# A state-space convolution with an MLP on one core: one PSUM pool for all stages, the first MLP block's sums in the searched order, and a new order

## The chip, the core and the metric

One core of a Trainium2 chip runs the whole program. The metric is the time of one execution on the device in microseconds; lower is better. The engines are PE (matmul), DVE (vector), ACT (scalar), POOL (GpSimd) and SP, whose queue mostly issues transfers; each works through its own queue in order and waits on the others by semaphores.

## What is computed

Two layers on a sequence of 2048 rows with 512 channels, with a layer normalisation ahead of each.

```python
# A: diagonal state space, applied as a long convolution
dt = exp(log_dt); logdA = dt * (A_re + 1j*A_im)
K  = real(sum_n C[d,n] * exp(logdA[d,n] * l) * dt*B[d,n])      # 512 x 2048 filter
y  = irfft(rfft(u, 4096) * rfft(K, 4096))[:2048] + u * Dskip
h  = x + y(layernorm(x))
# B: MLP, F = 1376
out = h + gelu(layernorm(layernorm(h)) @ w1 + b1) @ w2 + b2
```

## The kernel before

The kernel never forms the filter by 128 x 2048 exponentials per channel. It builds two small tables per half of the channels, multiplies them into the filter, and does the Fourier transforms as matmuls with tables of sines.

Stages, in the order in which they begin:

- `params`, `tables`, `norm_in` (lines 322 to 789): sines and cosines in `M`, turned copies in `R` and `Rn` by transposing DMAs, the layer normalisation of `x` (`st` are its sums, `u` the normalised rows). Each of 16 row groups is multiplied by a block-diagonal table (`aps`, line 780), copied from PSUM to SBUF (`a`, line 784) and written to DRAM (`A_dram`, line 789).
- `exps`, `p_half`, `q_half` (602 to 691), once per half of the channels: exponentials on ACT into `Pt` (the tile `both`) and `Q`; phases by matmul (`pv`, `qv`), their sines on ACT (`s`, `sq`, line 118), products on DVE.
- `kgen` (694): four blocks per half, each of 128 small matmuls of 128x32 by 20 columns (line 707, `kps`), a copy on ACT (`ku`) and two sums on DVE (`near`, `far`). These go to DRAM and come back as `kt` (lines 732 to 739). The second half's exponentials write over what the first half's `kgen` reads.
- `x_load`, `x_stage` (792 to 825): `A_dram` is read back as `X` in four loads, and 16 steps of 8 matmuls (`xps`) finish its spectrum in place.
- `conv` (828): for each half 8 pairs of frequencies; 22 matmuls (`kfps`, lines 848 and 850), a copy (`kf`), four products on DVE (`pa`, `pb`), 8 matmuls (`zps`, 873 to 876), a copy (`z`), a write to DRAM (`Zd`) and a return in another layout (`both<-Zd`, line 888). The last pair of the second half is done in two parts.
- `early_rows` (955): the first 256 channels of the convolution's result, by `first_half` (line 930, `y`), with the input row added and sums for the normalisation (`first_sums`).
- `mlp` (987): four blocks of 512 rows. `y_mm` and `y_sums` do the other 256 channels; `scale` normalises (`y2`); `turn` transposes, in block 0 on PE (`tps`, line 1047) and later by DMA; `up` makes 11 pieces of the hidden layer (`h1ps`, line 1055: four matmuls, then the GELU on ACT, line 1057, into `hT`); `down` makes an output tile of 128 rows (`o2ps`, line 1067: 11 matmuls, then the residual add on DVE into `ot`, and a write). In block 0 the ups run twice over 256 columns, elsewhere once over 512.

What sets the order: everything ahead of `mlp` is recorded as steps in a planner (`Sched`, line 121), with an engine, a cost and dependencies each. The list `ORDER` (line 31), found by a search outside the program, says in which order the steps are issued; where a step may run on two engines (copies from PSUM on ACT or DVE), the lowest bit of the entry says on which. `mlp` is written out by hand and begins after the last step. Every wait between engines is put in by the framework from the tiles that the instructions touch.

PSUM has eight banks of 512 fp32 columns. Ahead of `mlp` one pool holds three buffers of two banks (tag `p`) and one (tag `q`, for `zps`). It is closed, and `mlp` opens its own pool, in which each of the tags `yps`, `o2ps`, `tps` and `h1ps` has two tiles in turn:

```python
pt = ps1.tile([P, 512], f32, name="h1ps")
...
pt = ps1.tile([P, 512 // parts], f32, name="o2ps", tag="o2ps")
```

Of the kernel before, what the change touches and what calls it, by code (L numbers as in the profile page):

```python
# [31 lines left out]
    110, 4, 24, 28, 8, 32, 40, 6, 38, 42, 36, 126, 140, 66, 142, 144, 44, 156, 68, 58, 124, 118, 22, 114, 86, 116, 88, 72, 296, 128, 278, 152, 164, 294, 280, 90, 276, 298,  # L32
    136, 292, 130, 70, 160, 122, 132, 284, 168, 120, 300, 112, 270, 138, 288, 48, 272, 178, 74, 290, 148, 286, 274, 134, 76, 60, 78, 80, 46, 166, 282, 50, 170, 188, 302, 10,
    52, 180, 174, 190, 54, 335, 434, 62, 56, 12, 173, 184, 82, 176, 254, 252, 92, 183, 262, 258, 476, 186, 470, 478, 464, 472, 480, 482, 94, 336, 466, 474, 338, 500, 454,
    468, 502, 340, 484, 96, 504, 192, 98, 488, 194, 494, 490, 100, 506, 486, 102, 508, 436, 496, 344, 106, 492, 438, 346, 456, 84, 348, 440, 414, 158, 405, 416, 350, 150,
    445, 512, 14, 418, 154, 162, 458, 420, 146, 554, 460, 510, 514, 548, 556, 524, 516, 498, 550, 536, 560, 558, 526, 552, 562, 530, 528, 196, 532, 538, 534, 198, 566, 564,
    518, 540, 568, 16, 200, 520, 446, 570, 19, 542, 202, 448, 522, 406, 544, 206, 450, 578, 408, 374, 208, 424, 212, 410, 546, 572, 224, 218, 230, 236, 242, 216, 584, 574,
    576, 222, 580, 582, 234, 586, 590, 588, 240, 246, 376, 592, 684, 718, 426, 379, 594, 380, 228, 698, 596, 704, 720, 700, 248, 354, 708, 384, 356, 686, 429, 696, 386, 314,
    688, 430, 359, 316, 716, 600, 714, 324, 364, 692, 326, 389, 694, 360, 734, 329, 366, 390, 710, 394, 330, 304, 706, 319, 690, 712, 369, 306, 320, 726, 396, 399, 370, 702,
    722, 756, 309, 400, 730, 728, 738, 310, 750, 724, 758, 736, 732, 740, 760, 744, 604, 752, 608, 786, 742, 612, 746, 792, 616, 754, 788, 780, 794, 748, 822, 782, 768, 796,  # L40
    824, 790, 810, 784, 770, 652, 826, 812, 798, 655, 800, 828, 772, 830, 656, 840, 658, 802, 620, 814, 842, 834, 623, 836, 804, 832, 680, 806, 844, 774, 682, 838, 628, 808,
    776, 624, 631, 846, 626, 778, 762, 848, 668, 764, 850, 636, 670, 766, 672, 638, 816, 674, 644, 882, 818, 852, 647, 820, 664, 854, 856, 892, 666, 676, 894, 640, 678, 896,
    660, 642, 858, 662, 898, 860, 862, 632, 900, 928, 634, 902, 864, 930, 932, 906, 648, 866, 910, 878, 650, 868, 870, 934, 912, 964, 936, 914, 938, 874, 916, 966, 946, 918,
    968, 920, 970, 948, 942, 1000, 972, 950, 886, 974, 924, 1054, 1002, 1004, 952, 978, 1056, 1036, 954, 1058, 956, 1006, 1038, 982, 1008, 1040, 1010, 960, 1060, 984, 1090,
    1062, 986, 1064, 1014, 1042, 1092, 1072, 1044, 1094, 1046, 1068, 1096, 1074, 1126, 1098, 1100, 1050, 988, 1128, 1076, 1018, 990, 992, 1104, 1130, 1078, 1020, 1108, 1080,
    1022, 1082, 996, 1132, 1110, 1162, 1134, 1112, 1136, 1024, 1164, 1086, 1180, 1026, 1166, 1028, 1114, 1182, 1184, 1116, 1144, 1140, 1118, 1168, 1146, 1032, 1171, 1186,
    1148, 1188, 1172, 1190, 1122, 1150, 1200, 1152, 1176, 1212, 1202, 1194, 1154, 1208, 1214, 1204, 1158, 1210, 1198, 1206
# [274 lines left out]
def tables(nc, S, K, cp, mp, cv, ct, c2, psp, dram):  # L322
# [117 lines left out]
    for k in (0, 8):  # L440
        def flip(k=k):
            nc.sync.dma_start_transpose(out=K.R[:, k:k + 8].rearrange("p k c f -> p (k c) f"), in_=K.M[:, 0, k:k + 8].rearrange("p k c f -> p (k c f)"))

        ends.append(S.dma("SP", 1.3, flip, [K.o_m[0]], 1.2, lat=1.8))
    K.o_rn = S.dma("SP", 1.3, lambda: nc.sync.dma_start_transpose(out=K.Rn[:], in_=K.Mn.rearrange("p k f -> p (k f)")), [K.o_mn], 1.2, lat=1.8)
# [3 lines left out]
def params(nc, S, K, cp, pp, sc, cv, psp, raws, ldt, dtb, grb):  # L449
# [76 lines left out]
    K.o_pl = S.dma("SP", 1.3, turn(src_p, K.PL, 0), [d1], 1.2, lat=1.8)  # L526
# [66 lines left out]
    for h in range(2):  # L593
        K.o_ql.append(S.dma("SP", 1.3, turn(src_q, K.QL, 16 * h), [d5, dq, q1], 1.2, lat=1.8))
# [36 lines left out]
def p_half(nc, S, K, sc, psp, hh):  # L631

    K.o_p, K.o_phs = [[], []], []
    for qd in range(2):
        S.group = f"p{hh}{qd}"
        for g in range(4):
# [22 lines left out]
            x = S.op("ACT", 0.94, sn, [p] + K.o_pe, acq="s", rel=[p], fun=AT["sin"][hh])  # L659
            K.o_p[qd].append(S.op("DVE", 1.23, mul, [x] + K.o_pe, rel=[x]))  # L660


def q_half(nc, S, K, sc, psp, hh):
    K.o_q = [[], []]
    for qd in range(2):
        S.group = f"q{hh}"
        for g in range(5):
# [22 lines left out]
            z = S.op("ACT", 0.94, sn, [x] + K.o_qe, acq="s", rel=[x], fun=AT["sin"][hh])  # L690
            K.o_q[qd].append(S.op("DVE", 0.63, mul, [z] + K.o_qe, rel=[z]))


def kgen(nc, S, K, cv, sc, psp, hh, KD):
    cell = {}
    ends, mm = [], []
    for s in range(2):
        for hv in range(2):
            def mms(s=s, hv=hv):
                Pt, Q = K.Pt, K.Q  # L700
                kps = cell[s, hv] = psp.tile([P, 2, 512], f32, name="kps", tag="p", bufs=PB)
                for i in range(16):
                    for u in range(2):
                        at = 64 * (i % 8) + 32 * u
                        for g in range(4):
                            c = 128 * s + 32 * g + 16 * hv + i
                            nc.tensor.matmul(kps[32 * g:32 * g + 32, i // 8, at:at + 20], lhsT=Pt[:, s, :, u, c - 128 * s], rhs=Q[:, :, u, c], start=True, stop=True, tile_position=(0, 32 * g))  # L707
# [14 lines left out]
            m = S.op("PE", 2.15, mms, K.o_p[s] + K.o_q[s], acq="p")  # L722
            mm.append(m)
            r = S.op("ACT", 0.45, real, [m] + ends, acq="ku")
# [230 lines left out]
def early_rows(nc, S, K, psp, zs, loads):  # L955
    for n in range(4):
# [8 lines left out]
        S.op("DVE", 1.3 if n else 2.8, lambda cell=cell, js=js: first_sums(nc, K, cell["y"][:], 0, js), [m, loads] + K.o_pr0, rel=[m])  # L965
# [21 lines left out]
def mlp(nc, tc, K, ZT, ov):  # L987
    with tc.tile_pool(name="m_sb", bufs=1) as sb, tc.tile_pool(name="m_rot", bufs=2) as rot, tc.tile_pool(name="m_ps", bufs=2, space=PSUM) as ps1:
        warm = sb.tile([1, 1], f32, name="warm")
        nc.scalar.activation(warm[:], K.ones[0:1, 0:1], ACT.Sqrt)  # L990

        def h_of(j, half=None):
            if j < 4:
                v = K.h0[:, j].rearrange("p (h c i) -> p h c i", h=2, c=2)
            else:
                v = K.X[:, j].rearrange("p c d -> p (c d)").bitcast(f32).rearrange("p (c h i) -> p h c i", c=2, h=2)
            return v if half is None else v[:, half]

        def as_h(ap):
            return ap.rearrange("p (h c i) -> p h c i", c=2, i=HW // 2)  # L1000

# [3 lines left out]
        y2, y2T, mv, yps = {}, {}, {}, {}  # L1005
        pairs = (slice(0, 2), slice(2, 4))

        def scale(tb, js):
            n = js.stop - js.start
            ve = rot.tile([P, 4], f32, name="ve2")  # L1010
            ts(nc, ve[:, 0:n], mv[tb][:, js, 1], 1.0 + EPS, ALU.mult, EPS * EPS, ALU.add)
            if not tb and not js.start:
                rs = rot.tile([P, 4], f32, name="rs2")
                nc.vector.reciprocal(ve[:, 0:n], ve[:, 0:n])
                nc.scalar.activation(rs[:, 0:n], ve[:, 0:n], ACT.Sqrt)
                nc.scalar.activation(warm[:], K.ones[0:1, 0:1], ACT.Gelu_apprx_tanh)
            else:
                rs = rsqrt(nc, rot, ve[:, 0:n], n, f"r{n}")
            for jj in range(js.start, js.stop):
                k = jj - js.start  # L1020
                ts(nc, as_h(y2[tb][:, jj, :]), h_of(4 * tb + jj), mv[tb][:, jj, 0:1], ALU.subtract, rs[:, k:k + 1], ALU.mult)

        def tiles(tb):
            mv[tb] = rot.tile([P, 4, 2], f32, name="mv2")
            y2[tb] = rot.tile([P, 4, 512], bf16, name="y2")
            y2T[tb] = rot.tile([P, 4, 4, P], bf16, name="y2T")

        def aggr(tb, js):
            for jj in range(js.start, js.stop):
                nc.vector.bn_aggr(mv[tb][:, jj, :], K.st0[:, 4 * tb + jj, 0:1 if tb else 2].rearrange("p h s -> p (h s)"))  # L1030

        def y_mm(tb, n, tag):
            yp = yps[tb, n] = ps1.tile([P, 2, HW], f32, name="y1", tag=tag)
            first_half(nc, K, yp, 1, slice(4 * tb + 2 * n, 4 * tb + 2 * n + 2))

        def y_sums(tb, n):
            first_sums(nc, K, yps[tb, n][:], 1, slice(4 * tb + 2 * n, 4 * tb + 2 * n + 2))
            aggr(tb, pairs[n])

        def turn(tb, js):  # L1040
            if tb:
                nc.sync.dma_start_transpose(out=y2T[tb][:, js].rearrange("p j c i -> p (j c) i"), in_=y2[tb][:, js].rearrange("p j d -> p (j d)"))
                return
# [198 lines left out]
```

## Time and profile before

| | |
|---|---|
| runs | 305.56 us median of 3 (304.06 to 309.19) |
| the profiled execution | 306.28 us, its span 304.5 us, mean granted PE clock 0.837 |
| busy in the span | PE 251.5 us (83%), DVE 196.6 (65%), ACT 182.7 (60%), POOL 29.7 (10%) |
| X's loads issued / all landed | 102.24 us / 117.1 us |
| first `kgen` on PE | 68.7 to 83.6 us |
| second exponentials on ACT | 85.4 to 101.4 us |
| last `z` copy begins / first `up` of the MLP begins | 201.54 us / 215.55 us |
| MLP: ups of block 0, downs of block 0 | 215.55 to 231.48, to 241.0 us |
| MLP: block 1, block 2, block 3 | to 261.1, to 281.4, to the end |

The page lists busy times first, then the span in 40 equal slices, whose digits are busy tenths. A PE that is counted busy need not run at its peak: the row PEclk beside it says what share of full clock was granted. Times after the chain's start are read from the chain of waits in order of time; the times of single instructions from the groups, where a mean is of one shape only if shapes are kept apart.

### The profile page before, as it was taken

What the parts mean: (1) busy time and instruction counts of PE and PEld (TensorE: products, weight loads), DVE (VectorE), ACT (ScalarE), POOL (GpSimd) and SP (SyncE); (2) the same over time, 40 slices, a digit from 0 to 9 for tenths busy, and PEclk for the clock granted to TensorE, in tenths of its full rate; (3) what the DMA queues carried; (4) which work ended last, traced back from release to release, by engine and by line L of the source; (5) the groups of instructions that cost most, each with busy time, mean ns of one, the idle gap of its engine ahead of it and who ended that gap; (6) DMA issues with size and microseconds to landing.
All of it is one profiled execution on the core that took longest, in us unless ns stands there. A gap on an engine that the chain in (4) does not pass through costs nothing.

```text
span 304.5 us, 5861 instructions
## 1 busy us (share of the span) xinstructions
PE 251.5 (83%) x2318; PEld 147.1 (48%) x2318; DVE 196.6 (65%) x419; ACT 182.7 (60%) x302; POOL 29.7 (10%) x87
## 2 busy tenths in 40 slices
PE   3284897868457589999999999984879999999995
PEld 3221222227411146888777777662565454444443
DVE  4999999996889799531555555657970265473012
ACT  4999899993099998664455555540673161450630
POOL 8100000004020000000411111124000000000000
PEclk9855557595555599999999999978599999999999
DMA  6600096907337692251773554742412104105001
GB/s 167 229 2 0 3 211 141 233 1 187 105 94 229 206 345 86 51 232 58 225 184 122 134 144 141 207 139 54 168 26 63 52 0 103 38 0 121 17 19 52
DMA packets 48901, 34.90 MB, mean 115 GB/s; under 512 B 26441, under 2 KB 46922, under 8 KB 48490
## 3 DMA queue, kind: packets, MB, share of 16 engines
q1 hardware_dynamic: 46810, 23.58, 28.6%
q0 software_dynamic: 2064, 10.95, 11.7%
q8 instruction: 18, 0.29, 0.4%
q14 instruction: 9, 0.07, 0.1%
HBM read 18.58 MB, written 11.22 MB: 98 GB/s over the span
## 4 chain that ended last, share of the span: by engine, by line
PE 58%; DVE 19%; DMA 9%; ACT 7%; issue 5%; SPq 1%; DVEq 0%; ACTq 0%; POOLq 0%
PE h1ps L1055 13%; PE kfps L850 13%; PE o2ps L1067 12%; PE kps L707 6%; DMA X<-A_dram 4%; DVE st L764 3%; DVE w L70 2%; ACT sq L118 2%; DVE both L70 2%; PE kfps L848 2%; DVE a L82 2%; ACT hT L1057 1%; PE aps L780 1%; PE zps L874 1%; DMA M<-in_A_A_re_dram 1%
## 5 line engine op out<-in xcount | busy, mean ns | idle before, releaser
L1057 ACT ACTIVATE hT<-h1ps,b_sb 128x512 bf16<-128x512 f32 (+3 forms) x55 | 32.8, 602 | 43.1 <-PE h1ps L1055 43.1
L1055 PE MATMUL h1ps<-y2T,early 128*128 128x512 bf16 (+3 forms) x220 | 44.5, 351 | 2.7 <-ACT y2T L80 1.8
L850 PE MATMUL kfps<-kt,M 128*128 128x256 bf16 x320 | 40.5, 274 | 0.0
L1067 PE MATMUL o2ps<-w_sb,hT 128*128 128x512 bf16 (+3 forms) x187 | 38.7, 366 | 0.0
L1055 PEld LDWEIGHTS <-early 128*128 128x128 bf16 (+1 forms) x220 | 23.0, 105 | 22.2 <-issue 6.7
L80 ACT CAST kf<-kfps 128x1024 bf16<-128x1024 f32 (+1 forms) x17 | 16.4, 963 | 27.4 <-issue 17.6
L850 PEld LDWEIGHTS <-M 128*128 128x128 bf16 x320 | 28.7, 98 | 6.8
L70 DVE TENSOR_TENSOR pa<-X,kf 128x1024 bf16<-128x1024 bf16 (+1 forms) x17 | 11.2, 661 | 29.1 <-ACT kf L80 29.1
L1067 PEld LDWEIGHTS <-hT 128*128 128x128 bf16 (+1 forms) x187 | 18.2, 98 | 19.7
L70 DVE TENSOR_TENSOR ot<-o2ps,X 128x512 bf16<-128x512 f32 (+1 forms) x13 | 8.4, 650 | 26.5 <-PE o2ps L1067 25.6
L707 PE MATMUL kps<-Q,both 128*32 128x20 bf16 x1024 | 18.6, 221 | 5.5 <-issue 5.5
L70 DVE TENSOR_TENSOR both<-s,both 128x1024 bf16<-128x1024 bf16 x32 | 20.3, 686 | 2.0 <-ACT s L118 2.0
L614 ACT ACTIVATE both<-th 128x256 bf16<-128x256 f32 x64 | 20.6, 400 | 1.7 <-DVE th L70 1.7
L707 PEld LDWEIGHTS <-both 128*32 128x32 bf16 x1024 | 17.8, 169 | 7.5 <-issue 6.7
L780 PE MATMUL aps<-u,BD 128*128 128x512 bf16 x32 | 15.4, 606 | 7.2 <-DVE u L775 5.1
L118 ACT ACTIVATE sq<-qv 128x1024 bf16<-128x1024 int16 x20 | 19.4, 1060 | 0.0
L80 ACT CAST z<-zps 128x1024 bf16<-128x1024 f32 (+1 forms) x16 | 15.8, 989 | 4.3 <-PE zps L876 3.5
L678 PE MATMUL qv<-rows 128*128 128x512 bf16 (+1 forms) x64 | 14.9, 358 | 3.3 <-ACT sq L118 1.9
L644 PE MATMUL pv<-rows 128*128 128x512 bf16 x32 | 13.3, 530 | 5.2 <-ACT s L118 3.6
L118 ACT ACTIVATE s<-pv 128x1024 bf16<-128x1024 int16 x16 | 15.8, 1032 | 0.1
L888 POOL DMA_DIRECT2D both<-Zd x17 | 8.5, 497 | 58.9 <-DMA Zd<-z 42.7
L711 ACT COPY ku<-kps 128x320 f32<-128x320 f32 x8 | 3.4, 446 | 17.6 <-PE kps L707 17.6
(212 smaller groups left out, 440.8 us busy)
## 6 DMA issues: line engine op xcount, KB each, us to landing
A_dram<-a SPq DMA_DIRECT2D x16, 256.0 KB, 2.6
X<-A_dram SPq DMA_DIRECT2D x4, 1024.0 KB, 9.6
Zd<-z SPq DMA_DIRECT2D x15, 256.0 KB, 3.0
both<-Zd POOLq DMA_DIRECT2D x15, 256.0 KB, 3.3
x<-in_A_u_dram SPq DMA_DIRECT2D x4, 512.0 KB, 7.6
rows<-in_A_u_dram POOLq DMA_DIRECT2D x1, 2048.0 KB, 9.1
out_dram<-ot SPq DMA_DIRECT2D x15, 128.0 KB, 1.7
Dp<-Dd POOLq DMA_DIRECT2D x6, 256.0 KB, 5.0
```

The lines of the kernel that those rows point to most:

```text
L70: nc.vector.tensor_tensor(out, a, b, op)
L80: nc.scalar.copy(out, in_)
L118: nc.scalar.activation(out, v.bitcast(i16)[..., 0:2 * n:2], ACT.Sin, scale=S2PI / 65536)
L614: nc.scalar.activation(K.Pt[:, :, k, 1, :], K.th[:, ds].rearrange("p (s c) -> p s c", s=2), ACT.Exp, scale=float(8 * k))
L644: nc.tensor.matmul(v[:, n], lhsT=K.PL[:, b, :], rhs=K.RP[:, 8 * n:8 * n + 8].rearrange("p i c d -> p (i c d)"), start=True, stop=True)
L678: nc.tensor.matmul(v[:, n], lhsT=K.QL[:, b + n, :], rhs=K.RQ[:, m0:m1].rearrange("p i c d -> p (i c d)"), start=True, stop=True)
L707: nc.tensor.matmul(kps[32 * g:32 * g + 32, i // 8, at:at + 20], lhsT=Pt[:, s, :, u, c - 128 * s], rhs=Q[:, :, u, c], start=True, stop=True ...
L780: nc.tensor.matmul(ps[:, h, :], lhsT=K.BD[:, h].rearrange("p a b -> p (a b)"), rhs=cell["u"][:], start=True, stop=True)
L850: nc.tensor.matmul(ps[:, k, c, :], lhsT=K.M[:, t, 2 * k2 + k, c, :], rhs=kt[:, t, :], start=(c == 1 and t == 0), stop=(t == 4))
L1055: nc.tensor.matmul(pt[:fs, 0:n].rearrange("p (a b) -> p a b", b=P), lhsT=K.w1_sb[:, dc, fc * P:fc * P + fs], rhs=y2T[tb][:, js, dc, :], st ...
L1057: nc.scalar.activation(hT[tb % 2][:fs, fc, cols], pt[:fs, 0:n], ACT.Gelu_apprx_tanh, bias=K.b1_sb[:fs, fc:fc + 1], scale=1.0)
L1067: nc.tensor.matmul(pt[:], lhsT=h[:fs, fc, jj * P:(jj + 1) * P], rhs=K.w2_sb[:fs, fc, d], start=(fc == 0), stop=(fc == NFC - 1))
```

## The change

- One PSUM pool. The planner's pool stays open to the end. `mlp` takes four tiles of two banks from it (`o2`, `h1` and `y` with tag `p`, `t` with tag `q`) and `bank()` hands out the two halves of a tile in turn, where it took a new tile from a pool before.
- The first MLP block's start moves into the planner (`first_block`): one group of `y` matmuls for its four row groups, the sums of the first pair of row groups, the sums of the second pair, the root on ACT with the two table loads, and the normalisation of both pairs. The load of ACT's table for the root becomes a step of its own that may come earlier.
- Each `kgen` block of 128 matmuls (256 instructions with the weight loads) becomes two steps of 64.
- The return of the first half's Z waits, in the plan, for all eight of these steps.
- The planner's costs of the transposing DMAs are other numbers.
- `ORDER` is a new list. In it all 16 `A_dram` writes and X's four loads stand ahead of the first `kgen`'s writes on SP; 12 of the 16 `a` copies are on ACT and 4 on DVE (before: 7 and 9); 12 of the 16 `x` steps stand ahead of the second half's phases; the second `kgen` is almost in one piece; the split pair of frequencies is the last of the second half; ACT's table for the root is loaded amid the spectra.
- `w2`'s tile is taken after the new tiles; its loads remain the last step of POOL's queue.

```diff
-def mlp(nc, tc, K, ZT, ov):
-    with tc.tile_pool(name="m_sb", bufs=1) as sb, tc.tile_pool(name="m_rot", bufs=2) as rot, tc.tile_pool(name="m_ps", bufs=2, space=PSUM) as ps1:
+def mlp(nc, tc, K, psp, ov):
+    with tc.tile_pool(name="m_sb", bufs=1) as sb, tc.tile_pool(name="m_rot", bufs=2) as rot:
...
+        for nm, tag in (("o2", "p"), ("h1", "p"), ("y", "p"), ("t", "q")):
+            v = psp.tile([P, 2, 512], f32, name="bank_" + nm, tag=tag, bufs=PB if tag == "p" else QB)
+            banks[nm] = [v[:, n] for n in range(2)]
+
+        def bank(nm):
+            l = banks[nm]
+            l.append(l.pop(0))
+            return l[-1]
...
-                tp = ps1.tile([P, 4, P], bf16, name="tps", tag="tps")
+                tp = bank("t").bitcast(bf16)[:, 0:512].rearrange("p (c i) -> p c i", c=4)
...
-            pt = ps1.tile([P, 512], f32, name="h1ps")
+            pt = bank("h1")
...
-                pt = ps1.tile([P, 512 // parts], f32, name="o2ps", tag="o2ps")
+                pt = bank("o2")[:, 0:512 // parts]
```

```diff
+def first_block(nc, S, K, psp, done, sines_done, rows):
...
+    def sums(n):
+        js = PAIRS[n]
+        first_sums(nc, K, cell["y"][:, js], 1, js)
+        variances(nc, K, K.T0, 0, js)
+        if not n:
+            nc.vector.reciprocal(K.T0.ve[:, js], K.T0.ve[:, js])
...
+    table = S.op("ACT", 1.4, table, sines_done)
+    y = S.op("PE", 1.75, mm, done, acq="p")
+    a = S.op("DVE", 1.8, lambda: sums(0), [y, rows], rel=[y])
+    b = S.op("DVE", 1.7, lambda: sums(1), [y, rows], rel=[y])
+    r = S.op("ACT", 0.35, root, [a, table])
+    S.op("DVE", 0.7, lambda: normed(nc, K, K.T0, 0, PAIRS[0], K.rs0), [r], lat=4.0)
+    S.op("DVE", 1.3, second, [b])
```

```diff
-                for i in range(16):
+                if not part:
+                    cell[s, hv] = psp.tile([P, 2, 512], f32, name="kps", tag="p", bufs=PB)
+                kps = cell[s, hv]
+                for i in range(8 * part, 8 * part + 8):
...
-            m = S.op("PE", 2.15, mms, K.o_p[s] + K.o_q[s], acq="p")
-            mm.append(m)
-            r = S.op("ACT", 0.45, real, [m] + ends, acq="ku")
+            m = S.op("PE", 1.08, lambda mms=mms: mms(0), K.o_p[s] + K.o_q[s], acq="p")
+            m2 = S.op("PE", 1.08, lambda mms=mms: mms(1), [m])
+            mm += [m, m2]
+            r = S.op("ACT", 0.45, real, [m2] + ends, acq="ku")
...
-        ends.append(S.dma("SP", 1.3, flip, [K.o_m[0]], 1.2, lat=1.8))
+        ends.append(S.dma("SP", 2.1, flip, [K.o_m[0]], 1.6, lat=0.8))
...
-    psp = front.enter_context(tc.tile_pool(name="ps", bufs=1, space=PSUM))
+    psp = ctx.enter_context(tc.tile_pool(name="ps", bufs=1, space=PSUM))
```

## The prediction, made before the changed kernel ran

> **What bounds the kernel now.** First the page: span, busy time, slices. Then the chain of waits in order of time, the groups with shapes kept apart, the instructions in order of time around 197 us, and a table of the granted clock in stretches of 2 us.
>
> ```profile
> span 304.5 us, 5861 instructions
> ...
> PE   3284897868457589999999999984879999999995
> ...
> ACT  4999899993099998664455555540673161450630
> ...
> PEclk9855557595555599999999999978599999999999
> ```
>
> Three parts: up to 118 us (slice 15) ACT and DVE are full and PE is held at half clock; from there to 197 us PE is full (filter spectra); from 215 us to the end PE is full again (MLP). Between the last two lie some 14 us of copies and round trips through DRAM.
>
> ```profile
> 225.09 0.61 PE h1ps L1055 x4
> 225.72 0.48 ACT hT L1057
> 226.25 0.61 PE h1ps L1055 x4
> ...
> 231.48 9.51 PE o2ps L1067 x44
> ...
> 244.10 3.53 PE h1ps L1055 x16
> ```
>
> Call the four matmuls of `up` with their GELU an up, the eleven of `down` with their residual add a down. The chain shows how far apart ups are kept: PE 0.61, ACT 0.48, PE 0.61, hand-overs of 0.02 and 0.04. That loop takes 1.16 us and advances two ups (eleven ups take 6.40), because up n waits for the GELU of up n-2: two PSUM buffers. Wide ups (512 columns) don't wait at all: 3.53 / 4 = 0.883 us each; a down takes 9.51 / 4 = 2.38.
>
> ```profile
> L1067 PE MATMUL o2ps<-w_sb,hT 128*128 128x512 bf16 x150 | 34.8, 379 | 0.0
> L1055 PE MATMUL h1ps<-y2T,early 128*128 128x512 bf16 x120 | 28.2, 378 | 0.0
> L1057 ACT ACTIVATE hT<-h1ps,b_sb 128x512 bf16<-128x512 f32 x30 | 20.6, 688 | 37.0 <-PE h1ps L1055 37.0
> ...
> L1057 ACT ACTIVATE hT<-h1ps,b_sb 128x256 bf16<-128x256 f32 x20 | 9.2, 474 | 5.2 <-PE h1ps L1055 5.2
> ...
> L70 DVE TENSOR_TENSOR ot<-o2ps,X 128x512 bf16<-128x512 f32 x11 | 7.6, 691 | 25.1 <-PE o2ps L1067 25.1
> ```
>
> Here are the prices: a wide matmul 378 ns from start to end (216 from start to start), a GELU 688 or 474 ns, a residual add 691.
>
> ```profile
> 197.19 0.69 DVE L82 CAST z<-zps 128x512 bf16<-128x512 f32 x1 [2.22 <-PE zps L876]
> ...
> 197.93 0.27 PE L873 MATMUL zps<-pa,R 128*128 128x256 bf16 x1 [0.78 <-DVE z L82]
> ```
>
> This pair decides the case. The last pair of frequencies is done in halves, and the halves of one `zps` tile lie in different banks. Still the matmul that writes the second bank waits 0.78 us until DVE has read the first. Two banks of one tile are not two buffers.
>
> ```profile
> 58.00:60.00 2.00, 2.00 (x8) 0.50 0.93 312
> 60.00:62.00 2.00, 1.55 (x12) 0.94 0.00 0
> ...
> 66.00:68.00 2.00, 1.62 (x5) 0.77 0.00 0
> ...
> 92.00:94.00 2.00, 1.55 (x4) 0.50 1.02 232
> ```
>
> Columns: PE busy, matmuls, clock, DMA. Half clock ends after 3 to 5 us of nearly dense matmuls (60 us) and comes back after a thin stretch (64 to 66 us). With PE busy for some two thirds or three quarters of the time at half clock (92 us) it stays.
>
> **The change, part by part.** Sums are against the profiled execution: 306.28 us, 1.8 above its span, 0.7 above the median of 305.56.
>
> *One PSUM pool.* `mlp` had five tags with two tiles each. Now it takes four two-bank tiles and hands out their slices in turn. In the built program of the changed kernel the first matmul of every up waits for the GELU of the up just before (before: two back), the first of every later down of a block for the add of the down just before, the second transposes for the copy of the first: as with `zps`. What was overlapped is now in series.
>
> Wide ups: a cycle is 3 x 0.216 + 0.378 + 0.02 + 0.69 + 0.05 = 1.79 instead of 0.883, +0.91 for ten waits in each of blocks 1 to 3. The four `y` groups (0.44) of blocks 1 and 2 now lie in the waits: -1.8. Together 27.3 - 1.8 = +25.5.
>
> Downs: 0.378 - 0.216 + 0.02 + 0.69 + 0.05 = +0.92 per wait, 12 waits = +11.0; the last half of the last, with its 0.42 add, +0.65. Together +11.7.
>
> Ups of block 0 (256 columns, 22 of them): at full clock a cycle is 1.16 instead of 0.58. But before, this stage starts at half clock and leaves it only after 4.9 us of dense matmuls (215.5 to 220.4). In series, at half clock, a cycle is 3 x 0.213 + 0.42 + 0.02 + 0.47 + 0.05 = 1.60, of which 0.85 is PE: 53%, less than in the 92 us row. So I take half clock throughout: 2 x (10 x 1.60 + 0.85) = 33.7, and 2.4 for the second transposes in series: 36.1 against 15.9 (215.55 to 231.48): +20.2. With full clock it would be 26.1: +10.2. The downs that follow start at half clock; until a dense stretch has raised it, about 1.3 of them (2.3 more each): +3, between 0 and +9.
>
> For blocks 1 to 3 the clock is the open point. In series at full clock PE streams 0.864 of 1.79 us, 48%. By the matmuls that the rows list, the stretch 60.3 to 63.7 us had some 45% and kept full clock; 46.6 to 50.0 had 41% of full-height matmuls and lost it. 48% is nearest to the first: full clock. At half clock a cycle is 3 x 0.427 + 0.63 + 0.76 = 2.67, +0.88 for 30 waits, and each block's downs start slowly, 3 x 3: +35. The Trainium skill, "TensorE: Matmul & The Clock Gate", section "A second HAM failure mode: psum-queue depth-cycling", says that small idle times between groups that cycle through PSUM make the clock fall and rise again. By that rule the +35 or a part of it comes; the two stretches just named leave it open, so it is a rival below.
>
> *First block's sums and normalisation in the order.* DVE now does the second pair's sums (0.69 + 0.75 + 0.33 + 0.17 = 1.9) ahead of the first pair's normalisation, and one group of 8 `y` matmuls replaces the first of 4 (0.61): +0.9 at half clock. The Gelu table load (1.28 at 212.91) covers part of it. First GELU input later by +2.5, between +0.5 and +4. The Sqrt table load moves into the spectra, where ACT is half idle (slices 16 to 25): nothing; without that cover 1.3.
>
> *New order, front.* All 16 `a` copies come before kernel generation ends, 12 on ACT (7 before), 4 on DVE (9). X's four loads are issued ahead of the `KD` puts on SP, at about 85 instead of 102.24 us, so the spectra of X are transformed during the second exponentials. But `kgen` of the first half starts 4 us later: DVE does four more `a` copies (1.22), six more `u` (0.37) and one product less (0.60) before it, while the two table sums (1.41, 1.57) move behind: +3.5. `aps`, `qv` stand between its blocks (3 us), so it ends near 90 instead of 83.6. The exponentials, which overwrite its inputs, end near 110 (101.4, +6.4, two X copies of 1.0 between). Then come 24 ACT pieces of about 1.0, then four `kps` blocks of 2.25: the second kernel generation ends near 144 instead of 145, with one `x` (0.87), one `kf` (2.82), one `z` (0.87) more done by then. From there PE is full in both. Gain 1 + 4.6, taken as -6. Bounds: PE's "issue" gaps inside `kgen` (5.5 us) and 3 more, -14; X's loads making those gaps longer, +4.
>
> *Halves of the filter blocks.* Same 128 matmuls per block; only what stands between changes, counted above: nothing. Without that cover, one more semaphore wait for each of eight blocks, below 0.5.
>
> *End of the spectra.* The split pair comes last in the changed order: kf copy 0.59 for 1.02, products 1.3 for 2.1: -1.5, bounds -2.5 and 0. *w2 later*: its load follows the last Z return as before, needed 20 us later: nothing. *Changed costs of the transposes* are the planner's numbers and issue nothing.
>
> Sum: -6 - 1.5 + 2.5 + 20.2 + 3 + 25.5 + 11.7 = +55.4; 306.3 + 55.4 = 361.7, say 361.
>
> **Rivals.** (1) The clock falls in the wide ups: 361 + 35 = 396, near 378 if in half of them. For it: 48% is close to what lost it. Against: 45% kept it. (2) The clock rises early in block 0: -10 - 3 = 348. For it: the table of 2 us has no row of 256-column groups in series. Against: 53%. (3) The other side: the waits don't bind, since the instruction that a wait names is over when PE comes to it. Then ups stay at 0.883 and 0.58, and only front, head and tail count: 306.3 - 6 - 1.5 + 2.5 = 301, with the best front 293. It decides if ups in blocks 1 to 3 start less than 0.9 us apart. Against: a GELU can't start before its own matmuls end, and `zps` shows such a wait bind. The Trainium skill, "PSUM — Partial Sum Buffer", section "PSUM bank collisions raise a hardware error", says that accesses of two engines to different banks don't collide; by that the chip needs none of these waits, but the built program has them, and the 0.78 us at `zps` stand. (4) Front worse than before by 4: 371, inside the range.
>
> **How the numbers follow.** Forecast 0.48; clock lower in wide ups 0.30; clock higher in block 0 0.14; waits that don't bind 0.08. Forecast alone: 352 to 371 (front -14 to +4). Leaving 0.08 below, and from rival (1) the uppermost part, above: 344 to 396. A measurement can tell about 2% (6 us) from no change: faster 0.03 and same 0.05 (rival 3 with best and usual front), slower 0.92, all other cases.
>
> **What would show it.** Chain after 215 us: PE, ACT, PE, ACT with x4 each, 1.79 apart for wide ups, 1.6 in block 0; PE waits for `hT` and `ot` of some 35 and 10 us in the table of waits; clock 0.5 in block 0, 1.00 in the later ups. X's loads near 85 us, the first `kgen` ending near 90, the second near 144. I am wrong if ups run 0.9 us apart, or if the front moves by over 14 us.

## The result, and the profile after

The changed kernel takes 371.9 us (median; 370.58 to 372.86) beside 304.81 us for the kernel before: ratio 1.221, 95% interval 1.2139 to 1.228. The forecast was 361, in a range of 344 to 396. The profiled execution took 371.24 us with a span of 369.4, so 64.96 more than the profiled one before.

The page of the changed kernel: span, PE and ACT in 40 slices, and the granted clock.

```profile
span 369.4 us, 5858 instructions
...
PE   4243978793888796899997556667776776676575
...
ACT  4997899962999961255556033332023103302310
...
PEclk9655568975599998699999955555999999999999
```

From the 23rd slice on (203 us: the head, then the MLP) PE is no longer at 9: it is at 5 to 7, and ACT beside it is at 0 to 3. Neither engine is full, so something alternates. The chain of waits in order of time (start, length, engine, tile, line) shows what:

```profile
220.54 1.02 PE bank_h L1106 x4
...
221.65 0.48 ACT hT L1108
...
222.17 1.02 PE bank_h L1106 x4
...
256.45 4.34 PE bank_o L1118 x11
...
260.82 0.70 DVE ot L71
...
261.56 2.55 PE bank_o L1118 x11
...
272.38 1.04 PE bank_h L1106 x4
...
273.44 0.70 ACT hT L1108
...
274.18 1.04 PE bank_h L1106 x4
```

Where a line `x16` of ups stood before, each up now stands alone and is followed by its GELU. Up to up is 1.58 us in block 0 (222.17 to 223.75) and 1.80 in block 1 (272.38 to 274.18); downs are 3.32 apart (261.56 to 264.88) instead of 2.38. The table of waits gives the sum of it (us in total, times, longest):

```profile
PE bank_h L1106 <- ACT hT L1108: 34.1, 50, 0.8
...
PE bank_o L1118 <- DVE ot L71: 9.9, 13, 0.8
```

And the table in stretches of 2 us (PE busy, matmuls, clock, DMA share, GB/s):

```profile
222.00:224.00 2.00, 1.26 (x6) 0.50 0.00 0
...
254.00:256.00 2.00, 1.44 (x7) 0.50 0.00 0
...
260.00:262.00 2.00, 1.22 (x6) 0.93 0.00 0
...
274.00:276.00 2.00, 1.48 (x9) 1.00 0.00 0
...
350.00:352.00 2.00, 1.02 (x4) 1.00 0.00 0
```

Block 0 runs its ups at half clock to the end; the first dense down brings the clock back, and the wide ups keep it.

Cut at the same events in both traces, the 65 us lie here:

| from, to | before | after | difference | forecast |
|---|---|---|---|---|
| start to last z copy (201.54, 203.91) | 201.54 | 203.91 | +2.4 | -7.5 |
| head: to the first up (215.55, 220.54) | 14.01 | 16.63 | +2.6 | +2.5 |
| ups of block 0 | 15.93 | 35.91 | +20.0 | +20.2 |
| downs of block 0 | 9.52 | 14.29 | +4.8 | +5.8 |
| ups of blocks 1 to 3 | 31.52 | 57.78 | +26.3 | +25.5 |
| downs of blocks 1 to 3, last half included | 29.17 | 38.15 | +9.0 | +8.9 |
| tail, and what lies outside the span | 4.59 | 4.57 | 0.0 | 0 |

The forecast column is the prediction's own sum, with its +11.7 and +3 for downs laid out by block. Only the first line is off by more than 1 us.

### The profile page after: what moved, and what is told of

Same layout as the page of the kernel before. It is cut to its first block, busy times and chain, and to the rows that moved or that the text cites. A ratio compares the mean times of both kernels' runs of the same rounds, so it can differ in the third digit from the quotient of the medians.

```text
span 369.4 us, 5858 instructions
## 1 busy us (share of the span) xinstructions
PE 262.7 (71%) x2318; PEld 150.8 (41%) x2318; DVE 201.5 (55%) x425; ACT 180.3 (49%) x299; POOL 29.5 (8%) x87
## 5 line engine op out<-in xcount | busy, mean ns | idle before, releaser
L1108 ACT ACTIVATE hT<-bank_h,b_sb 128x512 bf16<-128x512 f32 (+3 forms) x55 | 33.1, 602 | 98.6 <-PE bank_h L1106 98.6
L1106 PE MATMUL bank_h<-y2T,early 128*128 128x512 bf16 (+3 forms) x220 | 56.0, 389 | 35.4 <-ACT hT L1108 34.1
L1106 PEld LDWEIGHTS <-early 128*128 128x128 bf16 (+1 forms) x220 | 25.5, 116 | 64.5 <-issue 49.0
L1118 PE MATMUL bank_o<-w_sb,hT 128*128 128x512 bf16 (+3 forms) x187 | 42.8, 379 | 9.9 <-DVE ot L71 9.9
L71 DVE TENSOR_TENSOR ot<-bank_o,X 128x512 bf16<-128x512 f32 (+1 forms) x13 | 8.5, 650 | 51.2 <-PE bank_o L1118 51.2
L71 DVE TENSOR_TENSOR ot<-bank_o,h 128x512 bf16<-128x512 f32 x4 | 2.8, 692 | 39.2 <-PE bank_o L1118 39.2
L345 PE MATMUL v<-crow,three 1*128 1x512 bf16 (+1 forms) x12 | 7.1, 596 | 11.0 <-ACT M L119 5.9
L83 DVE CAST X<-xps 128x1024 bf16<-128x1024 f32 x12 | 14.3, 1217 | 0.6 <-PE xps L827 0.5
L680 PE MATMUL qv<-rows 128*128 128x128 bf16 (+1 forms) x64 | 11.8, 306 | 3.6 <-ACT sq L119 1.9
L71 DVE TENSOR_TENSOR Q<-sq,Q 128x1024 bf16<-128x1024 bf16 x20 | 13.4, 684 | 1.1 <-ACT sq L119 0.9
```

What stands on the lines that cost most here:

```text
L71: nc.vector.tensor_tensor(out, a, b, op)
L83: nc.vector.tensor_copy(out, in_)
L345: nc.tensor.matmul(v[:, k:k + step], lhsT=R[l][:], rhs=rhs, start=(i == 0), stop=(i == len(terms) - 1))
L680: nc.tensor.matmul(v[:, n], lhsT=K.QL[:, b + n, :], rhs=K.RQ[:, m0:m1].rearrange("p i c d -> p (i c d)"), start=True, stop=True)
L1106: nc.tensor.matmul(pt[:fs, 0:n].rearrange("p (a b) -> p a b", b=P), lhsT=K.w1_sb[:, dc, fc * P:fc * P + fs], rhs=T[tb].y2T[:, js, dc, :], ...
L1108: nc.scalar.activation(hT[tb % 2][:fs, fc, cols], pt[:fs, 0:n], ACT.Gelu_apprx_tanh, bias=K.b1_sb[:fs, fc:fc + 1], scale=1.0)
```

## Experiments: is it the shared tile?

The theory: two banks of one tile are one buffer to the program's waits, and these waits in series are the whole loss in the MLP. The rivals: the new order or the long-lived pool causes it; or the half clock does.

**Eight tiles of one bank in the changed kernel.**

```diff
-            v = psp.tile([P, 2, 512], f32, name="bank_" + nm, tag=tag, bufs=PB if tag == "p" else QB)
-            banks[nm] = [v[:, n] for n in range(2)]
+            banks[nm] = [ps1.tile([P, 512], f32, name=f"bank_{nm}{n}")[:] for n in range(2)]
```

(`ps1` is a pool of its own, opened after the front's is closed, as before the change.)

> The changed kernel with eight one-bank PSUM tiles in the MLP in place of four two-bank tiles; order, halves and head stay as changed. If the sharing of a tile by two banks is the whole loss of the MLP, the seven stages from the first up to the end fall back to the lengths they had before the change (ups of block 0 15.9 us, wide ups 0.883 us apart, a block of downs 9.5 us), 60 us in sum: 371.9 - 60 = 312 us, 1.02 of the kernel before, with PE's waits for hT and ot near zero. What is left over the kernel before, about 5 to 7 us, is then front and head. If something else of the change also slows the MLP (order of the steps, one pool for all, w2), it stays at 330 or more.

Measured: 309.56 us, ratio 1.016 (1.0091 to 1.0229). Its chain of waits, downs of block 1 and ups of block 2:

```profile
256.09 9.24 PE bank_o L1117 x42
265.33 2.73 PE bank_h L1105 x12
...
268.50 3.59 PE bank_h L1105 x16
```

The x12 and x16 are back. From the first up to the last add it takes 85.7 us (before 86.1, after 146.1). All of the MLP's loss went; the 4.7 us that remain over the kernel before are 2.5 at the last z copy and 2.2 in the head.

**The shared tiles alone, in the kernel before.** The same `bank()` over four two-bank tiles, in the MLP's old pool, old order, old head.

```diff
+        for nm in ("o2ps", "h1ps", "yps", "tps"):
+            v = ps1.tile([P, 2, 512], f32, name="bank_" + nm)
+            banks[nm] = [v[:, n] for n in range(2)]
...
-            pt = ps1.tile([P, 512], f32, name="h1ps")
+            pt = bank("h1ps")
```

> The kernel before with only one thing changed: its MLP takes four two-bank tiles and hands out their halves in turn. If the shared tile alone makes the loss, it becomes 304.8 + 60 = 365 us (1.20), with wide ups 1.80 to 1.86 apart and half clock through the ups of block 0. If the loss needs the new order or the pool that lives on from the front, it stays below 340.

Measured: 364.64 us, 1.1946 (1.1878 to 1.2014); first up to last add 145.6 us. The loss needs neither the new order nor the new pool.

**Two tiles for the ups only.**

```diff
+            if nm in ('o2', 'y', 't'):
+                v = ps1.tile([P, 2, 512], f32, name="bank_" + nm)
+                banks[nm] = [v[:, n] for n in range(2)]
+            else:
+                banks[nm] = [ps1.tile([P, 512], f32, name=f"bank_{nm}{n}")[:] for n in range(2)]
```

> The changed kernel with two separate tiles for the ups only; the downs, the y groups and the transposes still share a two-bank tile. The waits of the downs (twelve of 0.94 us and the last half's 0.65) and of the second transposes (about 1.2 in each half) stay, the ups go back to their former pace and the clock of block 0 rises with them: 371.9 - 48 = 324 us. If the share of the ups is smaller than their waits (because PE would be held by something else, such as the clock), it is 335 or more.

Measured: 322.71 us, 1.0588 (1.0524 to 1.0652). In its chain the downs stay in series:

```profile
285.11 2.55 PE bank_o L1121 x11
287.68 0.70 DVE ot L71
288.43 2.55 PE bank_o L1121 x11
```

3.32 from down to down, as in the changed kernel, while the ups of block 0 take 16.0 us again. So ups cost 49 us of the 65 and downs with the transposes 13 (322.71 - 309.56).

**One pool and two-bank tiles kept, but the two banks of a tile for different users.**

```diff
+        for a, b, tag in (("h1", "o2", "p"), ("h1", "o2", "p"), ("y", "t", "p"), ("y", "t", "q")):
+            v = psp.tile([P, 2, 512], f32, name="bank_" + a, tag=tag, bufs=PB if tag == "p" else QB)
+            banks[a].append(v[:, 0])
+            banks[b].append(v[:, 1])
```

> The changed kernel, still with one PSUM pool and four two-bank tiles in the MLP, but each tile's two banks go to two different users (one bank of ups with one of downs, twice; one of y with one of transposes, twice), so that two ups in a row lie in two tiles. If a wait per tile is the cause, and neither the pool nor the two-bank tiles as such, the MLP is as short as with eight tiles: ups wait for the GELU two back, 371.9 - 61 = 311 us or a little less than the run with eight tiles (309.6). If two banks of one tile disturb each other whoever uses them, it stays above 330.

(The two `y` groups of block 1, which borrowed the banks of `o2`, take those of `y` here.) Measured: 312.17 us, 1.0248 (1.0187 to 1.031). The tile as such is harmless, and so is one pool: what costs is two successive uses of one tile. What this leaves is at the edges, where the last up and the first down meet in one tile: in its chain PE waits for a GELU of 0.69 us at 257.53 and for an add of 0.70 at 267.97. First up to last add is 89.0 us.

## Experiments: why the front gained nothing

The first half of the forecast's miss: the second kernel generation was to end near 144 us and ended at 150.04. The instructions of PE there (start, length, shape, count, idle time before and its releaser):

```profile
138.37 1.31 PE L712 MATMUL kps<-Q,both 128*32 128x20 bf16 x65
140.41 2.33 PE L712 MATMUL kps<-Q,both 128*32 128x20 bf16 x129 [0.72 <-DVE Q L71]
145.06 2.32 PE L712 MATMUL kps<-Q,both 128*32 128x20 bf16 x128 [2.32 <-issue]
148.79 1.25 PE L712 MATMUL kps<-Q,both 128*32 128x20 bf16 x62 [1.41 <-issue]
149.97 0.39 PE L854 MATMUL kfps<-top,ones 2*128 2x256 bf16 x1
150.30 2.31 PE L856 MATMUL kfps<-kt,M 128*128 128x256 bf16 x10
```

Two idle times with no releaser (marked issue), 128 matmuls apart; and then `kfps` blocks of 2.31 us, where 1.27 is the length at full clock. What the transfers did from 142.7 to 145.1:

```profile
q1 hardware_dynamic: 496, 0.25, 34.2%
q0 software_dynamic: 35, 0.33, 33.8%
q8 instruction: 1, 0.02, 2.5%
```

The columns are packets, MB and the time they took. One packet of instructions (the page's 18 packets of queue 8 hold 0.29 MB, so 16 KB each) starts at 142.8 us, in the idle time, amid the load of `rows` (queue 0) and a Z store (queue 1). The Trainium skill, "Runtime: NRT & Kernel Launch", section "Instruction fetch mechanics", says that an engine's instructions come in blocks of 16 KB, 256 at a time, by an own DMA queue, mostly hidden. The size and the distance agree (128 matmuls with 128 weight loads), and so does the number: PE's 2318 matmuls and 2318 weight loads make 18.1 such blocks. If the idle time is this fetch, "mostly hidden" doesn't hold for matmuls that take 2.32 us for 128, beside loads. The kernel before has the same kind of idle time in its first kernel generation, where `kps` blocks also stand in a row (0.81, 3.60 and 1.13 us):

```profile
73.37 2.32 PE L707 MATMUL kps<-Q,both 128*32 128x20 bf16 x128 [0.81 <-issue]
79.29 2.32 PE L707 MATMUL kps<-Q,both 128*32 128x20 bf16 x128 [3.60 <-issue]
82.74 0.85 PE L707 MATMUL kps<-Q,both 128*32 128x20 bf16 x39 [1.13 <-issue]
```

In its second one the blocks start at 120.27, 127.04, 135.70 and 142.63, and PE shows no such idle time, though the load of `rows`, issued at 126.53, runs beside the second of them.

**The load of rows later** (on POOL's queue behind the `kt` loads).

```diff
+    move(898, 890)
```

> The changed kernel with the 2 MB load of rows moved behind the kt loads on POOL's queue, so that it starts near 155 us in place of 136.6. If that load starves PE in the second kernel generation (idle times of 2.32 and 1.41 us with no releaser, DMA over 0.9 busy), these go, the clock doesn't fall there (4.6 us of half clock after it, worth 2.3), and the last z copy comes 5 to 7 us earlier: 366 us. If the idle times have another cause, they stay and so does the time, 372.

Measured: 366.88 us, 1.2031 (1.1965 to 1.2097).

```profile
140.61 4.59 PE L712 MATMUL kps<-Q,both 128*32 128x20 bf16 x257 [0.72 <-DVE Q L71]
146.33 1.25 PE L712 MATMUL kps<-Q,both 128*32 128x20 bf16 x62 [1.13 <-issue]
```

The 2.32 are gone, 1.13 remain. But the clock still falls (0.86 in the stretch from 142 to 144 us, 0.50 to 152), so the last z copy comes only 1.65 us earlier, not 5 to 7. Even that is not sure: the profiled executions with the changed front unaltered (the changed kernel and the runs on banks, head and dense matmuls) have it between 201.5 and 206.5. Counted from the start of the exponentials (the load of ACT's table ahead of them, 90.99 in the changed kernel), which takes the first kernel generation's varying idle time out, they have 111.9 to 115.5 us and this kernel 111.1. The medians differ by 5.0 us, the profiled executions by 3.7. Of these the last Z store and return are 1.5, and they vary by as much (6.2 to 8.3 us from the last z copy to the `y` matmuls over all runs); the MLP is 0.6. The total came as expected, its parts did not.

**The `kps` tiles apart**, with one `zps` group and one `kfps` block between them, rows' load where it was.

```diff
+    move(864, 862)
+    move(866, 864)
+    move(868, 866)
+    move(932, 868)
...
+    move(980, 876)
+    move(982, 980)
+    move(878, 982)
+    move(880, 878)
```

> The changed kernel with the six half blocks of the last three kps tiles in the second kernel generation no longer in a row: each tile's two halves come together, and one zps group and one kfps block that followed them stand between the tiles; the load of rows stays where it is. If PE's idle times there (2.3 and 1.4 us) come from instructions that arrive too late for matmuls of 18 ns each, and the clock's fall at 144 us from three thin blocks in a row, then both go: less idle time between 138 and 152 us, clock 1.00 or half for a shorter time, the last z copy 4 to 6 us earlier, 366 to 368 us in all. If the order of these steps does not matter (the load alone starves PE), it is 371 to 373.

Measured: 368.15 us, 1.2079 (1.2022 to 1.2137), and for the wrong reason: an idle time of 3.13 us, now in the middle of a tile (at 142.4, rows' load running), 112.9 us from the start of the exponentials to the last z copy, where the changed kernel has 112.9 too. All but 0.4 of the 2.5 us by which its profiled execution is shorter lie behind the last z copy. So this edit alone doesn't help: the load is a cause, and this spacing doesn't hide it. Nor does it keep the clock, though PE is busy without a gap from 145.56 to 158:

```profile
152.00:154.00 2.00, 2.00 (x110) 1.00 0.03 8
154.00:156.00 2.00, 2.00 (x12) 0.57 0.20 62
```

**X's loads later.**

```diff
+    move(612, 604)
+    move(616, 612)
+    move(620, 616)
+    move(624, 620)
```

> The changed kernel with X's four loads moved behind the KD puts on SP's queue. If these loads (1 MB each, from 86 us) starve PE in the first kernel generation, its idle time of 3.9 us goes and it ends near 87 in place of 90.5; X then starts near 92, the spectra of X begin some 6 us later and hold up the first sines: 372 to 375 us in all. If the idle time has another cause it stays, and the time is 376 or more.

Measured: 372.79 us in one execution. The idle time of 3.84 us in the first kernel generation stays with X's loads at 92 us, so they don't cause it. X later puts the last z copy 5.0 us later (208.89; 118.2 us from the start of the exponentials, beside 111.9 to 115.5 above), though the total hides that: the return was 1.8 us shorter and the MLP 1.2. So the early load by itself is a gain, as the prediction had it.

**The Dp loads later** (with the combined kernel below as its base). Dp are tiles of factors for the tables `M`, spread over the partitions by six loads of 256 KB from `Dd` in DRAM. Dd's store, the six loads and the first products come behind X's first load.

```diff
+    move(202, 612)
+    move(242, 202)
...
+    move(246, 602)
+    move(216, 246)
+    move(240, 216)
```

> The combined kernel with one more move: the store of Dd, the six Dp loads (256 KB each, on POOL's queue from 80 us) and their first products come behind X's first load, so that the Dp loads fall to some 88 to 98 us. If these loads make the instructions of the first kernel generation late (idle 4.1 us ahead of its last 57 matmuls), the idle time shrinks to about 1 us, the first kernel generation ends near 87.5 in place of 90.7, and the exponentials start 3 us earlier. DVE's Dp products then end some 6 us later and hold up its X copies, so the whole gains 0 to 3 us: 298 to 301. If the idle time stays at 3 us or more, the Dp loads are not its cause, and the time is 301 to 305.

Measured: 312.86 us, 1.0245 (1.0209 to 1.028).

```profile
82.89 2.32 PE L712 MATMUL kps<-Q,both 128*32 128x20 bf16 x128 [0.58 <-issue]
86.34 1.18 PE L712 MATMUL kps<-Q,both 128*32 128x20 bf16 x57 [1.13 <-issue]
```

The idle time ahead of the last 57 shrank from 4.1 to 1.13 and the exponentials began 3.2 us earlier (88.0), while X's loads, issued from 83.66 on, ran beside it. In the runs that leave these loads where they were it is 2.5 us or more, so it goes with the Dp loads, or with the store and products that moved along. Yet the whole lost 11.7 us. DVE waited 10.02 us for Dp at 98.71, its X copies ran to 122, and ACT's table for the sines came at 121.35 in place of 110.36. I had put that at no more than the gain.

## Experiments: head, clock, and all together

**The second pair's sums behind the first pair's normalisation.**

```diff
+    move(1238, 1242)
```

> The changed kernel with the second pair's sums put behind the first pair's normalisation, as before the change; the one group of eight y matmuls stays. By the sum, the sums of the second pair (1.9 us on DVE) leave the path to the first up and the Sqrt and the Gelu table load (1.5 us) take a part of their place: the first up 1 to 1.9 us earlier after the last Z return (8.7 us before), the whole 370 to 371. If the order on DVE did not matter, the distance stays at 8.7.

Measured: 365.9 us in one execution. From the first `y` matmul after the last return to the first up 7.32 us in place of 8.66: 1.34, within the 1 to 1.9 expected. The other 4 us of the total are front (last z copy 2.4 earlier, its idle time in the first kernel generation 2.50 in place of 3.88), a shorter return (0.7) and a shorter MLP (0.9), which the edit doesn't touch.

**Dense matmuls ahead of the first ups**, in the changed kernel; their result isn't read.

```diff
+        for n in range(11):
+            nc.tensor.matmul(banks["t"][0], lhsT=K.ident[:], rhs=K.w1_sb[:, 0, 0:512], start=True, stop=True)
```

> The changed kernel with eleven more matmuls of 512 columns, whose result nobody reads, on PE between the y groups and the first transposes (PE is idle there from 214.9 to 218.0), so that the first ups meet a clock that has risen. If the clock follows how densely PE streams, ups in series at full clock (1.15 us apart with 0.43 of PE's columns, 37%) lose it again within some 3 to 7 us, and the time falls by 2 to 3 us, to 369. If a clock that has once risen stays, 22 ups gain 0.42 each and the first down 2: 360 us. If the clock does not rise at all, 372.

Measured: 367.83 us (median; 362.82 to 369.08). The profiled execution took 367.17 us; the table in stretches of 2 us tells more:

```profile
216.00:218.00 2.00, 0.82 (x9) 1.00 0.40 154
218.00:220.00 2.00, 1.19 (x8) 1.00 0.00 0
220.00:222.00 2.00, 0.90 (x6) 0.91 0.00 0
222.00:224.00 2.00, 1.44 (x8) 0.50 0.00 0
```

The clock rose before the first up, held for three ups (1.2 us apart) and fell. In the clock records of these traces a state lasts a whole multiple of 3.41 us; the last step at full clock here, 218.24 to 221.65, is that of the three ups. Half clock in block 0 is thus not only a state the kernel happened to start in: three narrow ups in series lost full clock, and the nineteen behind them didn't bring it back. The gain from it is three ups and a transpose, some 2 us.

**All that helped, in one kernel**: banks of a tile for different users, with ups and downs alternating over the two tiles; rows' load late; `kps` tiles apart; the second pair's sums later; six dense matmuls.

```diff
+            for l in (("h1", "o2") if nm in ("h1", "o2") else (nm,)):
+                banks[l].append(banks[l].pop(0))
+            return banks[nm][-1]
```

> All that helped, together: the halves of a tile given to different users, with ups and downs alternating over the two tiles through every block, so that no edge waits (MLP some 86 us from the first up, as before the change), rows' load later and the kps tiles apart (some 6 us less before the last z copy), the second pair's sums behind the first pair's normalisation (1.3 to 2 less), and six matmuls of 512 columns ahead of the transposes for the clock (0 to 2 less). From the 309.6 us of the run with eight tiles: 309.6 - 6 - 1.5 - 1 = 301 us, 0.99 of the kernel before. If the gains of the front do not add up (the two edits there remove the same idle times), 304 to 306.

Measured: 301.17 us, 0.9872 (0.9847 to 0.9897): 1.3% below the kernel before. The interval excludes 1, but the difference is under the 2% that the prediction counts as a change. First up to last add 84.8 us, no wait at the edges. In the second kernel generation:

```profile
142.00:144.00 2.00, 2.00 (x128) 1.00 0.48 135
144.00:146.00 2.00, 2.00 (x27) 1.00 0.44 139
146.00:148.00 2.00, 2.00 (x74) 1.00 0.00 0
```

No idle time and full clock; the last z copy begins at 197.88, 106.7 us after the start of the exponentials (112.9 in the changed kernel, 111.1 with rows' load late, 112.9 with the tiles apart; 107.0 in the run that follows, which has the same front). Neither edit frees the stage alone, and both together do.

**The same without the six matmuls.**

> The combined kernel without the six matmuls of 512 columns ahead of the transposes. If the clock needs that dense stretch to be full at the first up, the first eleven ups start at half clock (7.6 to 8.0 us in place of 6.4), the first transposes too: 1.5 to 2 us more, 302.5 to 303. If the y groups alone raise the clock, 301.

Measured: 302.68 us, 0.9925 (0.989 to 0.9959). The first eleven ups take 8.05 us in place of 6.45: the 1.5 us expected.

## Why the prediction was right, and where it was not

- *Ups and downs in series, one PSUM pool*: right, mechanism and size. Per up 1.80 for 1.79 in block 1; 1.86 in blocks 2 and 3, where GELUs start 0.06 later after PE's end (+0.8 in sum). Waits 34.1 and 9.9 us, forecast 35 and 10. That the shared tile is the whole of it is shown from both sides: 312 expected and 309.6 measured without it, 365 and 364.6 with nothing but it.
- *Half clock in block 0*: right (36.1 forecast, 35.9 with the transposes). *Clock start of the downs*: the first down took 4.34 for 2.38, +2.0, forecast +3.
- *Rival 1, clock lower in wide ups*: no. With PE streaming 46 to 48% of the time (0.864 of 1.86 or 1.80 us) the clock kept 1.00 from 262 us to the end. What the Trainium skill, "TensorE: Matmul & The Clock Gate", section "A second HAM failure mode: psum-queue depth-cycling", tells of another kernel, that such cycling makes the clock fall and rise, doesn't show here at this share; in the narrow ups of block 0 (53% at half clock, 37% at full) the clock did stay low or fall.
- *Rival 2, clock up early*: no; even when it was raised on purpose it fell. *Rival 3, waits that don't bind*: no. *Rival 4, a worse front*: this one came, within its bounds.
- *Front, -6, and end of the spectra, -1.5*: wrong; +2.4 together. X's loads (86.26 for 85), the end of the first kernel generation (90.5 for 90) and of the exponentials (109.2, with one X copy behind them 110.1, for 110) came as said. The step that failed is "the second kernel generation ends near 144" and "from there PE is full in both". The sines ended at 137.8, not 134: ACT idles 3.7 us between the 24 pieces, waiting for PE. Then 3.7 us of idle time that I had counted only as a possible gain in the first kernel generation came in the second one as well: 150.04 (two of the eight half blocks ran before the sines' end, which takes some of this back). And PE was full after it but at half clock to 154.5: two `kfps` blocks in 4.76 us for 2.72. Of the 9.9 us missed, these are 6.0 and 2.0. The remaining 1.9 is open: PE idles 1.19 and 1.36 us around the split pair, which I have not tested apart.
- *Head, +2.5*: +2.6; its DVE part was 1.34 when undone.
- *Halves of the filter blocks, w2 later, at nothing*: no run has the halves alone undone. That three tiles' `kps` stand in a row is part of the front's miss, but whole blocks stand in a row too, in the first kernel generation of the kernel before, so the halves are not shown to be its cause; spacing the tiles gains only together with the later load. w2 cost nothing that shows.

## What to carry over

If two buffers are slices of one tile, look in the built program at which instruction the writer waits for: a wait per tile turns a double buffer into a single one, and here each such wait cost the whole consumer, 0.9 us times 42, and the clock where the matmuls are narrow. Give the two banks of a tile to users that don't follow each other, and the same space works. Size an expected gain at the stage's end only after asking what will run beside the work that moved: here streams of 20-column matmuls, next to the load of `rows` or of Dp, stood still for 2.3 to 4.7 us at a time.

## What the runs showed beyond that

- PE stops without a releaser in streams of 20-column matmuls while some big loads run: 2.3 to 4.7 us at a time. Moving rows' 2 MB took 2.32 us away, moving the six Dp loads 3.0 of 4.1; moving X's 4 MB changed nothing. That instructions arrive late is inferred from the packet in the idle time, from the number of packets and from the moves; it was not measured by itself.
- A PE that is counted busy for 2.00 of 2.00 us with 20-column matmuls lost full clock (142 to 144 us with rows' load late, behind a stretch with 1.39 of 2; just after 154 us with the tiles apart, behind a stretch with 2.00 of 2). With dense 256-column blocks between the tiles it kept 1.00 in the combined kernel and lost it in the run with the tiles apart, so what decides stays open. The small matmuls themselves don't depend on it: 128 take 2.33 us at clock 1.00 (138.60 us, combined kernel) and 2.32 at 0.50 (145.06 us, changed kernel).
- Wide matmuls in series with their GELU, PE streaming for under half of the time, kept full clock for some 90 us, with the denser downs between them.
